# Attention's recurrence in steps of 64 tokens, with all its products in 64x64 quarters of TensorE

## The chip, the cores and the metric

The kernel runs on one core of a Trainium2 chip. The metric is device time in microseconds (us). Of one execution there is also a hardware profile: its span runs from the program's first instruction to its last, and its own time is a little longer than the span.

## The reference

Two blocks follow each other. The first is linear attention with a decay per head (batch 4, 8 heads, 768 tokens, 64 channels a head), the second mixes tokens by a Fourier transform, adds, normalizes, and applies a two-layer MLP. Everything is float32. The part that the change touches is the first block:

```python
for b in range(nb):                       # blocks of 64 tokens
    intra = np.einsum('bhic,bhjc->bhij', qb, kb) * Dmask[None]     # lam ** (i - j), 0 above the diagonal
    intra = np.einsum('bhij,bhjd->bhid', intra, vb)
    inter = np.einsum('bhid,bhde->bhie', qb * lam_pow[None], kv_state)
    out[:, :, sl] = intra + inter
    kb_dec = kb * rev_pow[None]
    kv_state = lam_block[None, :, None, None] * kv_state + np.einsum('bhsd,bhse->bhde', kb_dec, vb)
```

The block length is a matter of arithmetic only: the same outputs come from blocks of 128 tokens. The second block is `u = x + real(fft2(x))`, then `u + relu(norm(u) @ w_ch1) @ w_ch2` with a hidden width of 2048.

## The kernel before

The program is written with a planner: Python emits instructions in an order of priority, and the planner issues on each engine whatever its own estimates of times say is ready, in that priority. `tc.keep_in_program_order` ("pinned") puts an instruction behind the one emitted just before it on the same engine, whatever the estimates say.[...] Generators yield estimated durations, and `weave` uses these to interleave attention, the Fourier part, weight loading and the MLP.

**Front (0 to about 360 us).** Attention goes batch by batch through `attn(b)`, in six chunks of 128 tokens. `attn_in` loads k, q and v of a chunk (L263), scales k by the decay on GpSimd (`kd`, L270), transposes k and q on TensorE (L274, L279) into `kT` and `qT` (ScalarE copies L276, L281), and forms `qs`, q times powers of the decay (VectorE, L285). `attn_out` does the recurrence in four products on TensorE:

- scores, L298: kT by qT for two heads at a time, on 64 rows by 128 columns of the array (two row tiles);
- states, L315: kd by v, 128 rows by 64 columns (two column tiles), added into the running state `st` after a scaling on GpSimd (L319, L320);
- state by qs ("inter"), L328: 64 by 64, the diagonal pair of quarters;
- v by masked scores ("intra"), L332: two column tiles, onto the same PSUM tile as inter.

VectorE multiplies the scores by the decay mask (`sc`, L302). ScalarE copies the result out (`oT`, L335); it is transposed back (L348) and goes on to the Fourier part. Batch 0 also builds a token-reversed copy in `ds` (L341, L390).

Attention's PSUM tiles share a pool of five banks (`psum_a`): scores take two (`pss`), states one (`pu`), the result one (`po`), transposes one each.

The chunks of batches 0 and 1 run beside the conversion of the MLP weights from float64 words (VectorE L217 to L225, ScalarE L216 and L218); those of batches 2 and 3 run beside the plain MLP (first layer L636, second layer L650).

**Late part (about 430 us to the end).** The remaining MLP rows are computed in pairs of row groups by a Strassen-like scheme with seven products a level. `inputs(j)` forms sums of a pair's input tile `ur` on VectorE, B12 at L796 and t1 at L799 among them. `place_sums_w` loads seven stored sums of weights back into the weight tiles (`w<-sd` and `w1s<-sd`, L745); `load_three` loads other stored sums (`tx`, L760), `load_u` the inputs (`ur`, L751), all on SyncE's (SP's) DMA queue. `deep_second(j, k)` are the second layer's seven products (TensorE L1038, read out at L1046 on VectorE and L1044 on ScalarE), `deep_first` the first layer's (L968).

Of the kernel before, what the change touches and what calls it, by code (L numbers as in the profile page):

```python
# [76 lines left out]
def kernel(  # L77
# [13 lines left out]
    DFF = moe_w_ch1.shape[1]  # L91
    C = 128
    NC = S // C
# [63 lines left out]

    decay = const.tile([C, H, C], F32, name="decay")
    for h in range(H):
        scan(decay[:, h, :], lamb[:, h:h + 1].broadcast_to([C, C]), ident, 0.0, op0=ALU.mult, op1=ALU.add)  # L160

    lamq = const.tile([128, HP], F32, name="lamq")
    for hi in range(2):
        nc.vector.tensor_copy(lamq[HD[hi]], lamb[HD[hi], hi::2])
    qpow = const.tile([128, HP, C], F32, name="qpow")
    for hp in range(HP):
        scan(qpow[:, hp, :], lamq[:, hp:hp + 1].broadcast_to([128, C]), ident, 1.0, op0=ALU.mult, op1=ALU.bypass)
    spow = qpow[:, :, C - 1:C]
    kpow = decay[:, :, C - 1:C].broadcast_to([C, H, D])

# [4 lines left out]

    st = [const.tile([128, HP, D], F32, name=f"st{i}") for i in range(2)]

# [81 lines left out]
    def attn_in(b, c):  # L259
# [6 lines left out]

        kd = None
        if c < NC - 1:
            kd = new(at, [C, H, D], "kd")
            nc.gpsimd.tensor_tensor(kd, kt, kpow, op=ALU.mult)  # L270

# [9 lines left out]
        nc.scalar.copy(qT, ptq)  # L281
        qs = None
        if c > 0:
            qs = new(at, [128, HP, C], "qs")
            nc.vector.tensor_tensor(qs, ptq, qpow, op=ALU.mult)  # L285
        ins[b, c] = kT, qT, qs, kd, vt
        yield 1.2

    def attn_out(b, c, head):
# [4 lines left out]
        mm = nc.tensor.matmul  # L294
        pss = [psum_a([C, HP, C]) for _ in range(2)]
        for hp in range(HP):
            for hi in range(2):
                mm(pss[hi][:, hp, :], lhsT=kT[HD[hi], hp, :], rhs=qT[HD[hi], hp, :], start=True, stop=True)  # L298
        sc = []
        for hi in range(2):  # L300
            t = new(at, [C, HP, C], "sc", bufs=3)
            nc.vector.tensor_tensor(t, pss[hi], decay[:, hi::2, :], op=ALU.mult)  # L302
            sc.append(t)
# [3 lines left out]


        s_old, s_new = st[(c + 1) % 2], st[c % 2]
        if not last:  # L310
            pu = psum_a([128, HP, D])
            for hp in range(HP):
                for hi in range(2):
                    h = 2 * hp + hi
                    mm(pu[HD[hi], hp, :], lhsT=kd[:, h, :], rhs=vt[:, h, :], start=True, stop=True)  # L315
            if c == 0:
                nc.vector.tensor_copy(s_new, pu)
            else:
                nc.gpsimd.tensor_tensor(s_new, s_old, spow.broadcast_to([128, HP, D]), op=ALU.mult)  # L319
                nc.vector.tensor_tensor(s_new, s_new, pu, op=ALU.add)  # L320
            yield 0.9


        po = psum_a([128, HP, C])
        if c > 0:
            for hp in range(HP):
                for hi in range(2):
                    mm(po[HD[hi], hp, :], lhsT=s_old[HD[hi], hp, :], rhs=qs[HD[hi], hp, :],  # L328
                       start=(hp == 0), stop=False, skip_group_check=True)
        for hp in range(HP):  # L330
            for hi in range(2):
                mm(po[HD[hi], hp, :], lhsT=vt[:, 2 * hp + hi, :], rhs=sc[hi][:, hp, :],  # L332
                   start=(c == 0 and hp == 0), stop=(hp == HP - 1), skip_group_check=True)
        oT = new(at, [128, HP, C], "oT")
        nc.scalar.copy(oT, po)  # L335
        if b in TURNED:

            if c == 0:
                nc.scalar.copy(first, po[:, :, 0:1])
            elif c > 1:  # L340
                nc.scalar.copy(oTs[b][:, :, 0:1], po[:, :, 0:1])  # L341
        yield 2.0
# [44 lines left out]
        if c > 0:  # L387

            oTs[b] = new(fp, [128, DM + 4], "ds")[:, 0:DM].rearrange("p (h c) -> p h c", h=HP)
            tc.keep_in_program_order(nc.scalar.copy(oTs[b][:, :, C - 1:0:-1], po[:, :, 1:C]))  # L390
        if last:
# [381 lines left out]
    def inputs(j):  # L773
# [21 lines left out]
        B11, B12, B21, B22 = (r[:, :, k::2, m:m + 128] for k in range(2) for m in (0, 128))  # L795
        V.tensor_tensor(B12, B22, B12, op=SUB)  # L796
        yield 0.0
# [224 lines left out]
    def deep_second(j, k):  # L1022
# [32 lines left out]
        if k == 0:  # L1055
# [3 lines left out]
            part_sum(V, h["a11"], h["s1"], h["a11"], SUB)  # L1059
            if j == DEEP - 1:  # L1060
                place_sums_w()
        elif k == 1:
            V.tensor_tensor(y11, y11, T, op=ADD)  # L1063
            add_u(y11, y11, 0, 0)
        elif k == 2:
            if j < DEEP:
                split(h["a22"])
            h["s4"] = h["a12"]
            part_sum(V, h["a12"], h["a12"], h["s2"], SUB)
        elif k == 3:  # L1070
            V.tensor_tensor(y22, y22, T, op=ADD)
            add_u(y21, y22, 1, 0)
            add_u(T, T, 0, 1)
            add_u(y22, y22, 1, 1)
        elif k == 4:
            V.tensor_tensor(y22, y22, y12, op=ADD)
            V.tensor_tensor(y12, y12, T, op=ADD)
        elif k == 5:
            store(*who[1][1], yt[:, 1, 1])
        else:  # L1080
            store(*who[0][1], yt[:, 0, 1])
            store(*who[1][0], yt[:, 1, 0])
            store(*who[0][0], yt[:, 0, 0])
# [181 lines left out]
```

## Time and profile before

| what | us |
|---|---|
| median of three runs | 803.37 |
| the three runs | 800.59, 803.37, 805.32 |
| profiled execution, own time | 800.95 |
| its span | 799.0 |
| TensorE busy | 768.3 |
| VectorE busy | 587.6 |
| ScalarE busy | 217.4 |
| GpSimd busy | 195.0 |

In the profile's rows a line such as L298 names the line of the kernel, `out<-in` the tiles, and `64*128` the rows and columns of the array that a matmul uses. Each float32 matmul leaves two records[...].[...] how fast matmuls follow one another is read from the starts. The granted clock of TensorE was 0.998 over the span.

### The profile page before, as it was taken

The page shows a single profiled execution, that of the slowest core. Times are in us where ns is not written, and L with a number is a line of the kernel's source. Part 1 is how long each engine was busy: PE and PEld are TensorE (multiplying, and loading weights), DVE is VectorE, ACT ScalarE, POOL GpSimd, SP SyncE. Part 2 cuts the span into 40 slices and gives each one's busy share as a digit, 9 for nine tenths or more (in the row PEclk, how much of TensorE's full clock was granted, in tenths as well). Part 3 has the DMA queues.
Part 4 walks back from the last instruction along what each step waited for, and adds up shares of the span by engine and source line. Part 5 has one row for each costly group of instructions (what it writes and reads, how often), then busy time and mean ns, then how long its engine had stood idle before and what let it go on. Part 6 is the DMA issues. An engine that isn't in the chain of part 4 may idle for free.

```text
span 799.0 us, 14578 instructions
## 1 busy us (share of the span) xinstructions
PE 768.3 (96%) x5616; PEld 642.5 (80%) x5616; DVE 587.6 (74%) x1148; ACT 217.4 (27%) x512; POOL 195.0 (24%) x196
## 2 busy tenths in 40 slices
PE   6989999999999999999999999999999999999996
PEld 5768766758675766767846889988899999999995
DVE  6899889675843572246698998769886699758983
ACT  3765443324431221221201221022210342024300
POOL 3213230011111020121003960279204101230021
PEclk9999999999999999999999999999999999999999
DMA  9979724238842137443232375345945555455442
GB/s 229 258 157 246 199 80 130 87 59 214 209 128 87 39 67 154 103 126 100 53 66 93 144 239 159 101 166 194 341 135 148 163 179 177 128 173 187 129 123 77
DMA packets 152331, 116.80 MB, mean 146 GB/s; under 512 B 113998, under 2 KB 113998, under 8 KB 152262
## 3 DMA queue, kind: packets, MB, share of 16 engines
q1 hardware_dynamic: 147120, 103.39, 46.2%
q0 software_dynamic: 2112, 6.69, 2.5%
q10 hardware_dynamic: 3030, 5.78, 2.1%
q8 instruction: 45, 0.74, 0.4%
q14 instruction: 24, 0.20, 0.1%
HBM read 83.58 MB, written 32.25 MB: 145 GB/s over the span
## 4 chain that ended last, share of the span: by engine, by line
PE 77%; DVE 11%; DMA 5%; issue 4%; ACT 1%; POOL 1%; POOLq 0%; ACTq 0%; SPq 0%; DVEq 0%
PE p L1038 20%; PE p L883 12%; PE p L968 11%; PE pm L650 10%; PE pm L636 8%; PE pa L332 3%; PE pa L516 3%; PE pa L298 3%; DMA x<-xb,ix 2%; PE pa L328 2%; DMA w<-sd 1%; PE pa L274 1%; PE pa L315 1%; DVE sc L302 1%; PE pa L348 1%
## 5 line engine op out<-in xcount | busy, mean ns | idle before, releaser
L636 PE MATMUL pm<-ut,w 128*128 128x256 f32 x512 | 119.2, 382 | 0.0
L650 PE MATMUL pm<-w,hr 128*128 128x512 f32 x256 | 115.8, 597 | 0.1
L636 PEld LDWEIGHTS pm<-ut,w 128*128 128x128 f32 x512 | 94.4, 190 | 15.4 <-issue 3.6
L650 PEld LDWEIGHTS pm<-w,hr 128*128 128x128 f32 x256 | 46.6, 190 | 49.5 <-issue 48.0
L1052 POOL TENSOR_TENSOR y<-y,u 128x512 f32<-128x512 f32 x12 | 18.8, 1568 | 200.8 <-DVE y L1063 159.0
L1038 PE MATMUL p<-tx,sx 128*128 128x128 f32 x416 | 54.9, 275 | 0.0
L1038 PEld LDWEIGHTS p<-tx,sx 128*128 128x128 f32 x416 | 50.6, 192 | 0.0
L883 PE MATMUL p<-ur,w 128*128 128x256 f32 x192 | 46.9, 379 | 0.1
L270 POOL TENSOR_TENSOR kd<-k,decay 128x512 f32<-128x512 f32 x20 | 22.6, 1130 | 97.0 <-PE pa L315 53.5
L1046 DVE TENSOR_TENSOR y<-p,y 128x128 f32<-128x128 f32 x92 | 25.4, 287 | 22.2 <-PE p L1038 15.8
L1044 ACT COPY y<-p 128x128 f32<-128x128 f32 x48 | 12.8, 266 | 104.1 <-PE p L1038 103.8
L883 PEld LDWEIGHTS p<-ur,w 128*128 128x128 f32 x192 | 36.3, 190 | 5.7 <-issue 0.5
L302 DVE TENSOR_TENSOR sc<-pa,decay 128x512 f32<-128x512 f32 x48 | 31.5, 684 | 8.7 <-PE pa L298 8.5
L1038 PE MATMUL p<-w,ha 128*128 128x128 f32 x288 | 37.4, 275 | 0.0
L298 PEld LDWEIGHTS pa<-qT,kT 64*128 64x128 f32 x384 | 26.0, 193 | 13.4 <-ACT qT L281 7.5
L332 PE MATMUL pa<-sc,v 128*64 128x128 f32 x384 | 32.2, 286 | 3.5 <-DVE sc L302 3.4
L644 ACT ACTIVATE hr<-pm 128x256 f32<-128x256 f32 x44 | 16.7, 385 | 68.7 <-PE pm L636 68.5
L1038 PEld LDWEIGHTS p<-w,ha 128*128 128x128 f32 x288 | 35.0, 192 | 0.2
L298 PE MATMUL pa<-qT,kT 64*128 64x128 f32 x384 | 30.7, 292 | 3.4 <-ACT qT L281 3.1
L550 POOL TENSOR_SCALAR ve<-mv 128x2 f32<-128x2 f32 x12 | 3.4, 286 | 123.0 <-DVE mv L547 123.0
L883 PE MATMUL p<-sx,w1s 128*128 128x256 f32 x128 | 32.9, 380 | 0.2 <-DVE sx L786 0.2
L332 PEld LDWEIGHTS pa<-sc,v 128*64 128x64 f32 x384 | 23.6, 140 | 11.3 <-DVE sc L302 5.5
(227 smaller groups left out, 1709.8 us busy)
## 6 DMA issues: line engine op xcount, KB each, us to landing
tx<-td SPq DMA_DIRECT2D x84, 256.0 KB, 2.9
raw<-in_moe_w_ch_dram SPq DMA_DIRECT2D x32, 512.0 KB, 5.1
tx<-sd SPq DMA_DIRECT2D x42, 256.0 KB, 2.7
sd<-tx SPq DMA_DIRECT2D x28, 256.0 KB, 2.0
k<-in_k_dram SPq DMA_DIRECT2D x24, 256.0 KB, 5.0
q<-in_q_dram SPq DMA_DIRECT2D x24, 256.0 KB, 5.9
v<-in_v_dram SPq DMA_DIRECT2D x24, 256.0 KB, 4.8
td<-tx SPq DMA_DIRECT2D x21, 256.0 KB, 2.0
```

The lines of the kernel that those rows point to most:

```text
L270: nc.gpsimd.tensor_tensor(kd, kt, kpow, op=ALU.mult)
L298: mm(pss[hi][:, hp, :], lhsT=kT[HD[hi], hp, :], rhs=qT[HD[hi], hp, :], start=True, stop=True)
L302: nc.vector.tensor_tensor(t, pss[hi], decay[:, hi::2, :], op=ALU.mult)
L332: mm(po[HD[hi], hp, :], lhsT=vt[:, 2 * hp + hi, :], rhs=sc[hi][:, hp, :], start=(c == 0 and hp == 0), stop=(hp == HP - 1), skip_group_chec ...
L516: mm = nc.tensor.matmul(ps[0:m, n, :], lhsT=piece(a, i, n), rhs=cs[0:rows, a, i in (2, 3), n, :], start=(a == 0), stop=(a == 1))
L636: nc.tensor.matmul(ps, lhsT=w1[:, c, 128 * fc:128 * fc + 128], rhs=ut[:, c, :], start=(c == 0), stop=(c == KO - 1))
L650: nc.tensor.matmul(ps, lhsT=hr[(fc - f0) // 4][:, fc % 4, 128 * i:128 * i + 128], rhs=w2[:, fc, :], start=(fc == f0), stop=(fc == f1 - 1))
L883: nc.tensor.matmul(ps, lhsT=s2.A[a][:, kt, 128 * i:128 * i + 128], rhs=U[b][:, kt, :], start=(first and kt == 0), stop=(kt == 1), skip_gro ...
L968: nc.tensor.matmul(ps[:, 128 * i:128 * i + 128], lhsT=ab[m][0][:, 128 * i:128 * i + 128], rhs=ab[m][1], start=(start and i == 0), stop=Tru ...
L1038: nc.tensor.matmul(ps[:, 0:HM // 2], lhsT=ab[m][0][i], rhs=ab[m][1][:, i, :], start=(start and i == 0), stop=(i == HF // 2 - 1), skip_grou ...
L1046: V.tensor_tensor(o, ps[:, 0:HM // 2], o, op=ADD)
L1052: nc.gpsimd.tensor_tensor(o, y, u, op=ADD)
```

## The change

The recurrence takes two steps of 64 tokens inside each 128-token chunk; loads, transposes and the copy of oT stay at 128.

- The decay tables cover 64 tokens, and `eye`, the sum of the identity's two halves, takes the identity's place in their scans. There are four state tiles instead of two.
- `kd` is also made for a batch's last chunk, and `qs` also for its first.
- States come first in `attn_out`: half-chunk s uses rows `HD[s]` of kd and v, so all four quarters of the array are used, and both states go into PSUM tiles `ps[0]` and `ps[1]`, beside the place for the scores. Each half's state is the old one scaled on GpSimd plus the sum on VectorE.
- Inter follows, one PSUM tile `po[s]` a half, every matmul pinned; then scores, of which only the two 64x64 blocks on the diagonal are computed, into the other half of `ps[hi]`; the first is pinned behind inter. The masked scores are half as wide.
- Intra uses four quarters as well; oT is copied in two halves, and batch 0's extra copies read oT instead of PSUM.
- In the late part, the sum B12 of `inputs` is pinned, and `place_sums_w()` is emitted after product 2 of the second layer of pair 1 instead of after product 0.

```diff
-    C = 128
+    C, SC = 128, 64
...
-    decay = const.tile([C, H, C], F32, name="decay")
+    decay = const.tile([C, H, SC], F32, name="decay")
     for h in range(H):
-        scan(decay[:, h, :], lamb[:, h:h + 1].broadcast_to([C, C]), ident, 0.0, op0=ALU.mult, op1=ALU.add)
+        scan(decay[:, h, :], lamb[:, h:h + 1].broadcast_to([C, SC]), eye, 0.0, op0=ALU.mult, op1=ALU.add)
...
-        qs = None
-        if c > 0:
-            qs = new(at, [128, HP, C], "qs")
-            nc.vector.tensor_tensor(qs, ptq, qpow, op=ALU.mult)
+        qs = new(at, [128, HP, 2, SC], "qs")
+        nc.vector.tensor_tensor(qs, ptq.rearrange("p h (s i) -> p h s i", s=2),
+                                qpow.broadcast_to([128, HP, 2, SC]), op=ALU.mult)
...
+        ps = [psum_a([128, 2, HP, SC]) for _ in range(2)]
+        for hp in range(HP):
+            for s in range(1 if last else 2):
+                for hi in range(2):
+                    h = 2 * hp + hi
+                    mm(ps[s][HD[hi], 1, hp, :], lhsT=kd[HD[s], h, :], rhs=vt[HD[s], h, :], start=True, stop=True)
+        states = [None if c == 0 else st[(2 * c) % 4]]
+        for s in range(1 if last else 2):
+            old, t = states[-1], st[(2 * c + s + 1) % 4]
+            if old is None:
+                nc.vector.tensor_copy(t, ps[s][:, 1])
+            else:
+                nc.gpsimd.tensor_tensor(t, old, spow.broadcast_to([128, HP, D]), op=ALU.mult)
+                nc.vector.tensor_tensor(t, t, ps[s][:, 1], op=ALU.add)
+            states.append(t)
+        yield 0.9
+
+        po = [psum_a([128, HP, SC]) for _ in range(2)]
+        pin = tc.keep_in_program_order
+        for s in range(2):
+            if states[s] is not None:
+                for hp in range(HP):
+                    for hi in range(2):
+                        pin(mm(po[s][HD[hi], hp, :], lhsT=states[s][HD[hi], hp, :], rhs=qs[HD[hi], hp, s, :],
+                               start=(hp == 0), stop=False, skip_group_check=True))
         for hp in range(HP):
             for hi in range(2):
-                mm(pss[hi][:, hp, :], lhsT=kT[HD[hi], hp, :], rhs=qT[HD[hi], hp, :], start=True, stop=True)
+                for s in range(2):
+                    i = slice(SC * s, SC * s + SC)
+                    m = mm(ps[hi][HD[s], 0, hp, :], lhsT=kT[HD[hi], hp, i], rhs=qT[HD[hi], hp, i], start=True, stop=True)
+                    if hp + hi + s == 0:
+                        pin(m)
         sc = []
         for hi in range(2):
-            t = new(at, [C, HP, C], "sc", bufs=3)
-            nc.vector.tensor_tensor(t, pss[hi], decay[:, hi::2, :], op=ALU.mult)
+            t = new(at, [C, HP, SC], "sc", bufs=4)
+            nc.vector.tensor_tensor(t, ps[hi][:, 0], decay[:, hi::2, :], op=ALU.mult)
             sc.append(t)
...
+        for hp in range(HP):
+            for s in range(2):
                 for hi in range(2):
+                    mm(po[s][HD[hi], hp, :], lhsT=vt[HD[s], 2 * hp + hi, :], rhs=sc[hi][HD[s], hp, :],
+                       start=(states[s] is None and hp == 0), stop=(hp == HP - 1), skip_group_check=True)
+        oT = new(at, [128, HP, C], "oT")
+        for s in range(2):
+            nc.scalar.copy(oT[:, :, SC * s:SC * s + SC], po[s])
...
-        V.tensor_tensor(B12, B22, B12, op=SUB)
+        tc.keep_in_program_order(V.tensor_tensor(B12, B22, B12, op=SUB))
...
-            if j == DEEP - 1:
-                place_sums_w()
         elif k == 1:
...
+            if j == DEEP - 1:
+                place_sums_w()
         elif k == 3:
```

## The prediction

> **What bounds the kernel now.** I read the page's busy times, then the busy times by stage, then the groups by shape, then the order of time inside one chunk.
>
> ```profile
> PE 768.3 (96%) x5616; PEld 642.5 (80%) x5616; DVE 587.6 (74%) x1148; ACT 217.4 (27%) x512; POOL 195.0 (24%) x196
> ```
>
> TensorE (PE) is nearly always busy, but an average hides stages, so I split the front, where attention runs, by time (columns: length, then busy us and instructions of PE, weight load, VectorE (DVE), ScalarE (ACT), GpSimd (POOL)):
>
> ```profile
> 5.00:95.00 90.00, 80.58 (x915) 65.53 (x916) 80.45 (x163) 51.22 (x114) 23.85 (x22) 1.00 0.87 218
> 95.00:140.00 45.00, 43.24 (x197) 30.67 (x198) 39.58 (x97) 17.94 (x43) 11.95 (x9) 1.00 0.41 130
> 140.00:250.00 110.00, 109.06 (x724) 77.89 (x723) 70.79 (x148) 39.64 (x87) 14.41 (x18) 1.00 0.53 137
> 250.00:360.00 110.00, 107.34 (x714) 74.67 (x713) 50.58 (x116) 21.06 (x54) 16.52 (x21) 1.00 0.40 95
> ```
>
> From 5 to 95 us, where batches 0 and 1 run beside the weight conversion, VectorE is as busy as TensorE (80.45 and 80.58 of 90): neither alone sets the pace. From 140 to 360 us, batches 2 and 3 run beside the MLP, TensorE has 216.4 of 220 us and VectorE 121.4. There a microsecond less on TensorE is a microsecond less. This is one full chunk of batch 3, in order of time (start, length first to last, engine, line, shapes, count):
>
> ```profile
> 331.74 1.16 PE L298 MATMUL pa<-qT,kT 64*128 64x128 f32 x16
> 332.83 0.69 PE L315 MATMUL pa<-v,kd 128*64 128x64 f32 x16
> 332.93 1.29 DVE L302 TENSOR_TENSOR sc<-pa,decay 128x512 f32<-128x512 f32 x2 [1.07 <-PE pa L298]
> 333.44 1.09 PE L328 MATMUL pa<-qs,st 64*64 64x128 f32 x16
> 334.13 0.41 DVE L320 TENSOR_TENSOR st<-st,pa 128x256 f32<-128x256 f32 x1
> 334.46 1.09 PE L332 MATMUL pa<-sc,v 128*64 128x128 f32 x16
> 334.69 0.62 POOL L319 TENSOR_TENSOR st<-st,qpow 128x256 f32<-128x256 f32 x1
> 335.49 0.66 PE L274 MATMUL pa<-ident,k 128*128 128x128 f32 x4
> 335.61 0.59 ACT L335 COPY oT<-pa 128x512 f32<-128x512 f32 x1 [3.92 <-PE pa L332]
> ```
>
> The four products take 335.49 − 331.74 = 3.75 us, without a gap: each VectorE step is covered by the next product. Two records stand for one f32 matmul (8 matmuls, 16 records). L315's records last 222 ns (its line's median), so its starts are spread over 0.69 − 0.22 = 0.47 us: 16 records in 8 steps of 58 ns, two at a time. The same sum gives L298 (record 272) 8 steps of 112 and L328 and L332 (269, 273) 8 steps of 109. A matmul on the whole array has no partner:
>
> ```profile
> 613.11 1.06 PE L968 MATMUL p<-ur,w 128*128 128x128 f32 x8
> 614.00 1.06 PE L1038 MATMUL p<-tx,sx 128*128 128x128 f32 x8
> ```
>
> 8 records in 0.89 us, one per 112 ns. So two column tiles (L315, L332), two row tiles (L298) and a diagonal pair (L328) all run at once already. Changing from one product to the next costs more than a step: L315's 0.61 us until L328 starts is 8 × 58 + 0.15; L328's 1.02 and L332's 1.03 are 8 × 109 + 0.15.
>
> [...]
>
> ```profile
> 43.84 1.06 POOL L270 TENSOR_TENSOR kd<-k,decay 128x512 f32<-128x512 f32 x1 [7.71 <-DMA k<-in_k_dram]
> 44.03 1.42 DVE L225 SCALAR_TENSOR_TENSOR w<-w,e 128x512 f32<-128x512 f32 x1
> ```
>
> L225 takes 0.685 us (median of its line), here 1.42.
>
> **The change part by part.** No row shows four quarters at once. I take four records per 58 ns, L315's step, because each pairing of rows and columns already overlaps fully.[...]
>
> *TensorE.* Per full chunk: states 32 records, 8 × 58 = 0.46; state times q uses the two diagonal quarters only, 16 steps × 58 = 0.93; scores 0.46; scores times v 0.46. That is 2.32. Inter and scores stand together, so I count three changes of mode where work lies between, 0.45: 2.77 against 3.75, saving 0.98. Batches 2 and 3, twelve chunks: before 12 × 3.75 − 2 × 1.02 (no L328 in a first chunk) − 2 × 0.61 (no L315 in a last) = 41.7; after 12 × 2.77 − 2 × 0.46 − 2 × 0.23 = 31.9. **−9.8 us.**[...]
>
> *New waits.* The second half's inter needs the state after the first half, and the second score bank is free only when VectorE has read the second state sum out of it, which waits for a GpSimd scaling of the first. With a handover of 0.05 us (L298's end at 332.90, L302 at 332.93): states end on TensorE at 0.52, the last record's tail at 0.69, add (L320, 0.41) to 1.13. Inter 1 may start at 1.19, inter 0 covers to 0.98: 0.2 open. GpSimd (L319, 0.62) and the second add end at 2.3; TensorE is done with inter 1 and half the scores at 1.9: 0.4 open. Then two score multiplies before scores times v; half size, L320's 0.41 each: 0.7 open. Sum 1.3 us per chunk, if nothing lies between. Behind the waiting matmul stands everything on TensorE that the planner put later. But each chunk has transposes of the next (L274 and L279, 0.93) and MLP matmuls (L650, 0.9), and the planner places them by its own estimates, leaving under 4 us of gaps in 220 now. I leave 0.2 a chunk open: **+2.4**, bounds 0 and 12 × 1.3 = 15.6.
>
> *VectorE.* Per batch: 12 score multiplies 0.684 to 0.41, −3.3; one more qs, +0.7; 11 state steps instead of 5, +2.5. About 0. GpSimd: six more scalings and one more kd per batch, 6 × 0.62 + 1.06 = 4.8, off every path except through the blocking: 9.6 us more in 5 to 95, where L225 alone loses 13 × (0.838 − 0.676) = 2.1 us to 23.85 us of GpSimd work. I take +2, bounds 0 and 9.6. ScalarE copies oT in two halves, 2 × 0.39 (L352's size) for 0.59: +0.2 per chunk, also ahead of the turned copies (L341, L390), which then read oT; covered by its idle time (51 of 90 us busy); uncovered, 12 × 0.2 = 2.4. The constants' twelve scans (L160 and L167, 0.4 each) halve and one add is new; VectorE waits 1.2 us for TensorE's first scores after them, so 0; uncovered, −2.2.
>
> *Batches 0 and 1.* TensorE again saves about 10 us, mostly into idle time since VectorE's work stays; where a chunk waits for TensorE it helps a little, and inter now stands ahead of the scores, so the wait for qs is uncovered. I take −1, bounds −6 and +6. With the blocking: **+1**.
>
> *Late part.*
>
> ```profile
> 579.01 0.69 DVE L796 TENSOR_TENSOR ur<-ur 128x512 f32<-128x512 f32 x1 [2.93 <-DMA ur<-utd]
> 579.62 0.28 DVE L1046 TENSOR_TENSOR t<-p,t 128x128 f32<-128x128 f32 x1
> ```
>
> VectorE sits 2.93 us before L796, whose input has not landed; the read of a product (L1046) is queued behind it and TensorE stands 1.44 us. Pinned, the sum goes to its place in the program, near its neighbour L799 at 606, long after the landing. place_sums_w moves seven 256 KB loads (about 0.4 us of issue each) two products later on SP's queue, past the two ur loads and the tx loads of those products, which come some 3 us earlier; the seven are needed near 613, so they have time. **−1.4**, bounds −1.6 and +2 (the seven then delay tx loads).
>
> Sum: −9.8 + 2.4 + 1 − 1.4 = −7.8. The profiled execution took 800.95 us (span 799.0), so about 793; it lies 2.4 under the median of the three runs, 803.37, which I carry over: **795.5**.
>
> **The rivals.** *The handover decides (slower).* If the planner's estimates of quarters are off, the chain PE, DVE, POOL, DVE, PE lies open. Per chunk it is 1.3 us plus about half a VectorE operation of queueing at each of three visits (0.3 each) = 2.2, less 0.98 saved = 1.2; over the 23 chunks after the first, −1.4 for the late part: +26 at worst, half of it +12, 815. It decides once more than 0.98 us a chunk stays open. For it: fixed order on TensorE, one shared bank. Against it: 1.8 us of other TensorE work per chunk. *Quarters don't run four at a time.*[...] 801 to 808, no change. *All is hidden:* stages 140 to 360 save the full 9.8 and batches 0 and 1 gain 5: 787.
>
> **How the numbers follow.** Measurements of this kernel can tell about 0.5% (4 us) from no change. Forecast with the hidden case, 786 to 799: 0.60. No change, 799.4 to 807.4 ([...]half the gain eaten): 0.20. Slower, 808 to 820: 0.20. The range for 8 in 10 is 786 to 812; the forecast's own is 787 to 800.
>
> **What would show it.** Right: records of the states, scores and last product averaging about 15 ns apart (0.7 us per 32), VectorE's score multiplies at 0.41, TensorE still above 98% busy from 140 on with the front ending 8 us earlier, L796's counterpart without an idle time. Wrong: 32 records spread over 0.8 us or more, or idle TensorE ahead of the second inter or the scores, released by the state's add, of over 1 us a chunk.

## The result, and the profile after

The changed kernel takes 835.52 us (median of 6 runs, 833.07 to 838.08) against 803.11 us (6 runs, 800.21 to 805.32): ratio 1.0415, 95% interval 1.0392 to 1.0438. It is slower by 32 us; the forecast was 795.5. The profiled execution took 838.08 us, with a span of 836.3. The times in the table of runs below are medians of executions in the chip's fast state; one of e4's four fell in its slow state and is left out.

The page of after, busy times and the row of granted clock (40 slices, tenths):

```profile
PE 779.9 (93%) x7152; PEld 651.9 (78%) x7152; DVE 587.1 (70%) x1177; ACT 220.0 (26%) x536; POOL 213.1 (25%) x224
PEclk9998899999999998999899999999999999999999
```

VectorE's sum has not moved (587.6 to 587.1), TensorE's share fell from 96 to 93%, and the clock now shows slices at eight tenths in the front.

Three points in time divide the loss: the first matmul of the plain MLP (L636 before, L643 after) comes at 120.6 us instead of 96.9, the first of the late part (L883, L890) at 469.2 instead of 428.9, and the end at 836.3 instead of 799.0. So batches 0 and 1 lose 24 us, batches 2 and 3 beside the MLP 16.6 us, and the late part gains 3.0. Busy time in the first two stages, before and then after (columns: window, length, busy us and count of PE, weight load, VectorE, ScalarE, GpSimd, clock, DMA share, GB/s):

```profile
5.00:96.90 91.90, 82.48 (x932) 67.42 (x933) 80.62 (x163) 52.02 (x117) 25.19 (x23) 1.00 0.88 219
96.90:428.90 332.00, 325.39 (x1886) 227.45 (x1885) 211.23 (x457) 85.45 (x204) 47.26 (x55) 1.00 0.42 109
```

```profile
4.70:120.60 115.90, 90.47 (x1701) 73.69 (x1702) 82.71 (x179) 53.25 (x129) 35.44 (x38) 0.91 0.70 173
120.60:469.20 348.60, 329.53 (x2655) 230.51 (x2654) 209.27 (x471) 86.83 (x216) 55.40 (x69) 0.98 0.40 104
```

VectorE does the same work in the first stage (80.62 and 82.71 us) but in 115.9 us instead of 91.9: its list is not what grew. GpSimd got 10 us more (25.19 to 35.44, still under a third of the stage), and TensorE's busy time rose by 8 us at a lower clock, to 78% of the stage: no engine is full, so they wait for each other. The clock is below 1 in both stages: 20.5 and 13.7 us in all at half clock, where the front of before has none.

This is one chunk of batch 2 of after, in order of time; it answers to the chunk shown of before:

```profile
259.65 0.69 PE L299 MATMUL pa<-v,kd 64*64 64x64 f32 x32
260.17 0.65 PE L317 MATMUL pa<-qs,st 64*64 64x64 f32 x16
260.45 0.42 DVE L307 TENSOR_TENSOR st<-st,pa 128x256 f32<-128x256 f32 x1 [0.50 <-PE pa L299]
260.54 1.06 POOL L270 TENSOR_TENSOR kd<-k,decay 128x512 f32<-128x512 f32 x1 [4.35 <-issue]
261.02 0.59 PE L317 MATMUL pa<-qs,st 64*64 64x64 f32 x13 [0.21 <-DVE st L307]
...
261.55 0.62 POOL L306 TENSOR_TENSOR st<-st,qpow 128x256 f32<-128x256 f32 x1
262.21 0.42 DVE L307 TENSOR_TENSOR st<-st,pa 128x256 f32<-128x256 f32 x1 [1.34 <-POOL st L306]
...
262.69 0.68 PE L323 MATMUL pa<-qT,kT 64*64 64x64 f32 x26 [0.79 <-DVE st L307]
```

The quarters run as fast as forecast: L299's 32 records lie in 0.69 us. But TensorE then waits 0.21 us before the second inter (L317) for the first state sum, and 0.79 us before the scores (L323) for the second one (L307), since the second score bank still holds it. That sum waits 1.34 us for GpSimd, which first does the next chunk's kd (L270, 1.06 us) and only then the scaling (L306). Nothing else of TensorE's list lies in the gap. The whole chunk, from this chunk's transposes of k at 256.16 to the next at 263.30, takes 7.14 us.

The waits of TensorE by what ended them (us in total, times, longest): the main ones of the first stage of before, then those of after before 120.6 us, then those from there to 469.2:

```profile
PE pa L298 <- ACT qT L281: 3.1, 7, 0.7
PE pa L332 <- DVE sc L302: 1.8, 5, 1.0
PE pa L328 <- DVE qs L285: 1.4, 2, 0.8
```

```profile
PE pa L323 <- DVE st L307: 6.1, 8, 1.5
PE pa L338 <- DVE sc L329: 4.9, 8, 1.1
...
PE pa L317 <- DVE qs L283: 2.9, 4, 1.9
PE pa L355 <- ACT ds L348: 2.4, 4, 0.8
PE pa L317 <- DVE st L307: 2.2, 5, 0.8
```

```profile
PE pa L523 <- DVE fe L482: 6.6, 3, 3.5
PE pa L323 <- DVE st L307: 5.7, 8, 0.8
...
PE pa L317 <- DVE st L304: 2.1, 1, 2.1
PE pa L317 <- DVE st L307: 1.2, 6, 0.2
```

To add up the stages I took all starts of TensorE's records in order. A distance of over 350 ns between two starts (700 ns after a 512-column record) counts as lost, less 0.42 ns for each column of the record, an allowance that I set; the rest counts as records. This sees more than the table of waits, which starts at a record's end: one of L299 lasts 0.22 us, while the next starts 15.4 ns later on average.

| TensorE, us | before | after |
|---|---|---|
| to the first MLP matmul: records / lost | 76.4 / 15.5 | 79.9 / 36.0 |
| from there to the late part: records / lost | 323.2 / 8.8 | 319.4 / 29.3 |

The lost time grows by 41 us and makes the whole loss of the front (40 us). The records' own time hardly changes (399.6 to 399.3 us over both stages): the quarters' gain is not to be seen. The allowance is about half of what the trace of before shows (L968 with 128 columns starts a record every 112 ns, L650 with 512 every 429); with the spacing that each line shows, the lost time grows by 38 us, which changes nothing in the reading.

### The profile page after: what moved, and what is told of

Same layout as the page of the kernel before. It is cut to its first block, busy times and chain, and to the rows that moved or that the text cites. A ratio compares the mean times of both kernels' runs of the same rounds, so it can differ in the third digit from the quotient of the medians.

```text
span 836.3 us, 17751 instructions
## 1 busy us (share of the span) xinstructions
PE 779.9 (93%) x7152; PEld 651.9 (78%) x7152; DVE 587.1 (70%) x1177; ACT 220.0 (26%) x536; POOL 213.1 (25%) x224
## 4 chain that ended last, share of the span: by engine, by line
PE 66%; DVE 14%; issue 7%; DMA 5%; POOL 5%; SPq 1%; ACT 1%; POOLq 0%; ACTq 0%; DVEq 0%
PE p L1045 20%; PE p L890 11%; PE p L975 10%; PE pm L643 7%; PE pm L657 5%; PE pa L523 3%; PE pa L338 2%; DMA x<-xb,ix 2%; POOL kd L270 2%; POOL st L306 1%; DVE stt L553 1%; PE pa L323 1%; DVE un L571 1%; POOL rs L558 1%; DVE st L307 1%
## 5 line engine op out<-in xcount | busy, mean ns | idle before, releaser
L657 PE MATMUL pm<-w,hr 128*128 128x512 f32 x256 | 118.6, 603 | 0.1
L643 PE MATMUL pm<-ut,w 128*128 128x256 f32 x512 | 118.2, 385 | 0.0
L643 PEld LDWEIGHTS pm<-ut,w 128*128 128x128 f32 x512 | 96.8, 192 | 16.2 <-issue 4.1
L270 POOL TENSOR_TENSOR kd<-k,decay 128x512 f32<-128x512 f32 x24 | 27.5, 1146 | 142.0 <-issue 49.8
L890 PE MATMUL p<-ur,w 128*128 128x256 f32 x192 | 46.7, 379 | 0.0
L323 PE MATMUL pa<-qT,kT 64*64 64x64 f32 x768 | 30.7, 240 | 11.9 <-DVE st L307 11.8
L283 DVE TENSOR_TENSOR qs<-pa,qpow 128x512 f32<-128x512 f32 x24 | 16.4, 685 | 35.6 <-ACT qT L281 35.3
L1053 DVE TENSOR_TENSOR y<-p,y 128x128 f32<-128x128 f32 x92 | 25.6, 286 | 22.5 <-PE p L1045 15.9
L890 PEld LDWEIGHTS p<-ur,w 128*128 128x128 f32 x192 | 36.4, 190 | 5.3 <-issue 0.5
L317 PE MATMUL pa<-qs,st 64*64 64x64 f32 x704 | 29.8, 226 | 11.1 <-DVE st L307 3.4
L317 PEld LDWEIGHTS pa<-qs,st 64*64 64x64 f32 x704 | 25.0, 137 | 18.8 <-issue 5.8
L306 POOL TENSOR_TENSOR st<-st,qpow 128x256 f32<-128x256 f32 x40 | 28.7, 717 | 41.0 <-DVE st L307 41.0
L323 PEld LDWEIGHTS pa<-qT,kT 64*64 64x64 f32 x768 | 24.6, 147 | 14.5 <-DVE st L307 14.5
L307 DVE TENSOR_TENSOR st<-st,pa 128x256 f32<-128x256 f32 x40 | 16.7, 418 | 26.9 <-POOL st L306 18.7
```

The costliest lines, as they stand in the source:

```text
L306: nc.gpsimd.tensor_tensor(t, old, spow.broadcast_to([128, HP, D]), op=ALU.mult)
L307: nc.vector.tensor_tensor(t, t, ps[s][:, 1], op=ALU.add)
L317: pin(mm(po[s][HD[hi], hp, :], lhsT=states[s][HD[hi], hp, :], rhs=qs[HD[hi], hp, s, :], start=(hp == 0), stop=False, skip_group_check=True))
L323: m = mm(ps[hi][HD[s], 0, hp, :], lhsT=kT[HD[hi], hp, i], rhs=qT[HD[hi], hp, i], start=True, stop=True)
L643: nc.tensor.matmul(ps, lhsT=w1[:, c, 128 * fc:128 * fc + 128], rhs=ut[:, c, :], start=(c == 0), stop=(c == KO - 1))
L657: nc.tensor.matmul(ps, lhsT=hr[(fc - f0) // 4][:, fc % 4, 128 * i:128 * i + 128], rhs=w2[:, fc, :], start=(fc == f0), stop=(fc == f1 - 1))
```

## The experiments

Label, time and ratio to the kernel before on the same chip (95% interval), and the time of the first MLP matmul, with the length of the stage from there to the late part. The last two columns come from one trace each. In e1, whose front is that of the kernel before, they are 1.7 us lower and 1.3 us higher than before (96.9 and 332.0), so differences of 1 to 2 us there tell nothing. Runs e11 to e16 were executed once each, for the times inside their traces, and have no line here.

| run | us | ratio | first MLP | stage after |
|---|---|---|---|---|
| changed kernel | 835.52 | 1.0415 (1.0392 to 1.0438) | 120.6 | 348.6 |
| e1_late_only | 799.57 | 0.9964 (0.9942 to 0.9985) | 95.2 | 333.3 |
| e2_kd_behind | 836.90 | 1.0413 (1.0370 to 1.0457) | 123.5 | 343.0 |
| e3_evac | 824.30 | 1.0244 (1.0162 to 1.0325) | 117.7 | 335.0 |
| e4_spread | 829.43 | 1.0290 (1.0230 to 1.0351) | 120.3 | 345.9 |
| e5_hybrid | 802.02 | 0.9989 (0.9973 to 1.0005) | 96.2 | 336.1 |
| e6_head_first | 822.07 | 1.0251 (1.0234 to 1.0268) | 115.5 | 335.7 |
| e7_piped | 828.76 | 1.0353 (1.0313 to 1.0393) | 116.4 | 341.7 |
| e8_piped_add | 829.08 | 1.0308 (1.0264 to 1.0352) | 119.5 | 340.4 |
| e9_filler | 849.14 | 1.0558 (1.0515 to 1.0601) | 134.7 | 345.5 |
| e10_piped_filler | 828.67 | 1.0317 (1.0275 to 1.0359) | 120.7 | 338.9 |
| e17_filler_128 | 834.83 | 1.0412 (1.0388 to 1.0436) | 119.3 | 345.5 |
| e18_piped_filler_256 | 832.89 | 1.0376 (1.0352 to 1.0400) | 123.0 | 343.2 |

My theory was a chain of handovers inside each chunk (TensorE, VectorE, GpSimd, VectorE, TensorE) that TensorE cannot cover. The rivals: four quarters lower the clock by themselves; the added GpSimd work only blocks VectorE; the number of PSUM banks; TensorE's half clock as a cost of its own.

**The late part alone.** The kernel before with this edit and the call of `place_sums_w()` two products later:

```diff
-        V.tensor_tensor(B12, B22, B12, op=SUB)
+        tc.keep_in_program_order(V.tensor_tensor(B12, B22, B12, op=SUB))
```

> The kernel before with only the late part's two edits (the sum B12 pinned, the stored weight sums loaded two products later). Theory 'late part as predicted, attention lost the rest': about 801.5, 1.4 to 1.6 us under the kernel before, B12 without an idle time ahead of it. Rival 'the late part's gain comes only with the new front': 803, no difference, and B12's wait goes to another row.

Measured 799.57 us, 2.9 us under the kernel before by the ratio (interval 1.2 to 4.7). The stretch from the first late matmul to L968's first fell from 184.2 to 182.5 us, in the changed kernel to 182.7. So the late part does what was forecast, 1.5 to 1.7 us of it visible in the trace, and the attention part lost the rest. **This is the version that beats both kernels**, the kernel before by 0.4%.

**Who holds the second score bank.** First only the order on GpSimd:

```diff
-        nc.gpsimd.tensor_tensor(kd, kt, kpow, op=ALU.mult)
+        tc.keep_in_program_order(nc.gpsimd.tensor_tensor(kd, kt, kpow, op=ALU.mult))
```

> The changed kernel with the scaling of k (kd) pinned on GpSimd behind the second scaling of the state, nothing else. Theory 'chain': a kd of 1.06 us stands ahead of the second scaling, so the second score bank opens about 1 us later than it could; with kd behind, the 14.2 us that TensorE loses before the scores fall under 5, and the time falls by 8 to 15 us, to 820 to 827. Rival 'quarters or clock': stalls are not what costs, time stays at 835 within 2 us. Rival 'GpSimd only moves the wait': kd comes late, TensorE waits before the states instead, 830 to 840.

The waits of TensorE over the front of that run:

```profile
PE pa L338 <- DVE sc L329: 9.7, 12, 1.6
PE pa L299 <- POOL kd L270: 9.5, 4, 4.8
...
PE pa L323 <- DVE st L307: 2.2, 10, 0.4
```

The scores' wait went as expected, from 11.8 to 2.2 us, and came back as 9.5 us before the states (kd is late now) and 4.8 us more before the last product. Time 836.90: the third theory named there was right. kd's place alone is not the cause; with either order someone waits. So GpSimd was taken out of TensorE's way:

```diff
-            else:
+            elif s == 0:
                 nc.gpsimd.tensor_tensor(t, old, spow.broadcast_to([128, HP, D]), op=ALU.mult)
                 nc.vector.tensor_tensor(t, t, ps[s][:, 1], op=ALU.add)
+            else:
+                u1 = new(at, [128, HP, D], "u1")
+                nc.scalar.copy(u1, ps[s][:, 1])
+                nc.gpsimd.tensor_tensor(t, old, spow.broadcast_to([128, HP, D]), op=ALU.mult)
+                nc.gpsimd.tensor_tensor(t, t, u1, op=ALU.add)
```

> The changed kernel, but the second state sum is copied out of PSUM by ScalarE as soon as it is there, and scaled and added on GpSimd from SBUF, so no bank waits for GpSimd. Theory 'chain': the wait before the scores goes (14.2 us to under 3), time 812 to 825; GpSimd does about 15 us more work, some of it against VectorE. Rival 'clock': the half-clock stretches come from the quarters themselves, clock stays at 0.98, 828 to 836. Rival 'blocking': GpSimd's added work slows VectorE, 835 or more.

The windows of that run:

```profile
4.70:117.70 113.00, 89.56 (x1700) 74.05 (x1701) 85.05 (x169) 56.14 (x137) 44.56 (x48) 0.88 0.70 176
117.70:452.70 335.00, 321.79 (x2655) 224.29 (x2654) 206.18 (x461) 90.42 (x226) 63.61 (x79) 1.00 0.42 109
```

The wait before the scores is gone from the second stage, its length falls from 348.6 to 335.0 us (before: 332.0), its clock is back at 1.00, and a dense chunk takes 5.94 us instead of 7.14. So in batches 2 and 3 the second score bank, with the half clock that came with it, is 13.6 of the 16.6 us (the edit also takes one add a chunk from VectorE). The rival "four quarters lower the clock by themselves" falls: this stage runs all its attention in quarters at full clock. So does "the added GpSimd work only blocks VectorE": GpSimd has more to do here than in the changed kernel, 63.61 against 55.40 us, in a shorter stage. But the first stage gained only 2.9 us: there the wait moved on to the masked scores (TensorE's longest wait before 117.7 us; last product, released by VectorE):

```profile
PE pa L343 <- DVE sc L334: 13.5, 9, 2.5
```

TensorE's order was then changed as well: inter of the first half, scores of one head of each pair, inter of the second half, scores of the other head.

```diff
+        for t in range(2):
...
+            hi = t
+            for hp in range(HP):
+                for s in range(2):
+                    i = slice(SC * s, SC * s + SC)
+                    m = mm(ps[1 - hi][HD[s], 0, hp, :], lhsT=kT[HD[hi], hp, i], rhs=qT[HD[hi], hp, i], start=True, stop=True)
```

> As the one before (second sum copied out by ScalarE), and TensorE's order is state times q of the first half, scores of one head of each pair (into the bank that ScalarE empties), state times q of the second half, scores of the other head. Theory 'chain': the wait before the second inter is covered as well; only the wait for the masked scores stays, 0.7 us a chunk: 803 to 815, clock back at 0.99 or more. Rival 'clock': still 828 or more with a clock of 0.98. Rival 'VectorE's queue in batches 0 and 1 is what costs': the gain is small before 140 us and the first MLP matmul still starts after 115 us, 820 to 828.

It missed: 829.43 us, with a clock of 0.969 in its trace. These are the numbers that the clock rival gave, but e3's second stage had already run quarters at full clock, and waits show here too. In the first stage the scores now wait for ScalarE's copy (L310), which stands in ScalarE's list behind other copies:

```profile
PE pa L343 <- DVE sc L334: 9.1, 8, 3.3
PE pa L328 <- ACT u L310: 6.0, 6, 1.7
```

In the second stage a matmul of the MLP waited 4.3 us for a weight tile, against 0.2 in e3. It seems that moving a few matmuls in one list shifted the others; that was not tried apart.

**Which batches.** Both recurrences in one kernel: batches 0 and 1 in steps of 128, batches 2 and 3 as in e3, the late part as changed.

```diff
+    OLD = (0, 1)
+    def attn_in(b, c):
+        return (in_128 if b in OLD else in_64)(b, c)
```

> Batches 0 and 1 take the recurrence of the kernel before (steps of 128), batches 2 and 3 that of the kernel with the second sum copied out by ScalarE; the late part as changed. Theory 'the early loss is the chain of handovers inside each chunk of batches 0 and 1': the first MLP matmul comes back to 94 to 99 us (120.6 changed, 117.7 with the copy), the stage from there to the late part stays at 333 to 337, no half-clock stretch in front; time 800 to 804. Rival 'tables, loads or weights delay the early part': first MLP matmul after 110 us, 815 or more.

The windows of that run:

```profile
5.00:96.20 91.20, 81.24 (x933) 65.94 (x934) 81.26 (x166) 51.79 (x117) 24.97 (x23) 1.00 0.89 222
96.20:432.30 336.10, 324.21 (x2655) 227.37 (x2654) 205.80 (x461) 90.16 (x225) 63.94 (x79) 0.99 0.42 108
```

As the theory expected: the first stage is back at 91.2 us and full clock, the second at 336.1, the time at 802.02. So the 24 us of the first stage come from the recurrence in batches 0 and 1; its batch 0 makes the token-reversed copy into ds from oT as the changed kernel does, so that copy is not the cause. The run also has decay tables of 128 tokens again. Those are made once, ahead of the first chunk, while the changed kernel falls behind through all twelve: the scores of the 1st, 4th, 8th and 12th chunk start 2.0, 8.4, 15.1 and 25.6 us later than before. And the new recurrence, freed of its bank wait, still gains nothing where TensorE is the limit: 336.1 against 332.0 us.

**What holds batches 0 and 1.** These kernels start from e3, but for the controls e14 and e15. First the next chunk's transposes between scores and last product:

```diff
         yield 1.5
+        yield from head
...
         oT = new(at, [128, HP, C], "oT")
...
         yield 2.0
-        yield from head
```

> The kernel with the second sum copied out by ScalarE, and the next chunk's loads and transposes emitted between the scores and the last product, so that they are at hand while VectorE masks the scores. Theory 'chain': the wait before the last product (15.0 us of lost time there) falls under 6, 812 to 817. Rival 'the planner had put the transposes there already': 822 to 826, the wait stays.

822.07 us, the rival's value, though not for its reason: the wait before the last product did go (16.2 to 0.6 us lost in the first stage), but TensorE then waited 8.3 us before q's transposes and 14.3 us, instead of 5.9, before the transposition of the result.

The states a whole chunk ahead, in PSUM tiles of their own, so that nobody waits for a state inside its chunk; e8 keeps the add on VectorE:

```diff
     def attn_in(b, c):
...
+        ps = [psum_a([128, HP, SC]) for _ in range(2)]
...
+        ins[b, c] = kT, qT, qs, vt, states
```

> One chunk of lead: the states of the next chunk are computed with its transposes, between the scores and the last product of this chunk, in PSUM tiles of their own; the second sum copied out by ScalarE. Then no state is waited for inside a chunk, and the masking of the scores is covered by transposes and states. Theory 'chain': lost time before inter, scores and last product under 10 us in all, clock 1.0 in front, first MLP matmul at 88 to 96, time 790 to 802. Rival 'quarters lower the clock': clock 0.98, 815 or more. Rival 'banks': two more PSUM tiles in flight of five make the transposes wait, 803 to 815.

> As the one before, but the second state is added on VectorE from PSUM after GpSimd's scaling, as in the changed kernel. Theory 'chain': nobody on TensorE waits for that add any more, so within 3 us of the one before, rather faster (GpSimd 15 us less work). Rival 'banks': the sum holds its bank until GpSimd is done, 5 us or more slower than the one before.

The order of e6 is in both. e7 missed: 828.76 us, the first MLP matmul at 116.4 instead of 88 to 96. e8 did as expected against e7: 829.08 us, so the sum that holds its bank for GpSimd costs nothing there. TensorE's waits in the first stage in e7, and in e13, the same kernel with seven PSUM banks for attention instead of five:

```profile
PE pa L279 <- DVE sc L336: 8.1, 6, 2.2
PE pa L362 <- ACT oT L350: 6.1, 6, 2.3
PE pa L362 <- ACT ds L356: 5.7, 4, 2.3
```

```profile
PE pa L346 <- DVE sc L336: 8.7, 7, 2.3
PE pa L362 <- ACT oT L350: 5.5, 6, 1.3
```

```diff
-    pa = psums.enter_context(tc.tile_pool(name="pa", bufs=5, space=PS))
-    pm = psums.enter_context(tc.tile_pool(name="pm", bufs=3, space=PS))
+    pa = psums.enter_context(tc.tile_pool(name="pa", bufs=7, space=PS))
+    pm = psums.enter_context(tc.tile_pool(name="pm", bufs=1, space=PS))
```

> The kernel with the states one chunk ahead, with seven PSUM banks for attention's tiles instead of five, and one instead of three for the MLP (which slows the MLP; only the time up to the first MLP matmul is compared, 116.4 with five banks). Theory 'banks took the place of the state chain': TensorE's 10 us of waits before q's transposes go to under 3 and the first MLP matmul comes at 95 to 106. Rival 'VectorE's and ScalarE's lists set the pace': 112 to 118.

> The changed kernel with seven banks for attention and one for the MLP. The scores still share their banks with the states, so theory 'handover inside the chunk' expects little before the first MLP matmul: 116 to 122 (120.6 with five). Rival 'it was the number of banks all the time': under 108.

> Control: the kernel before with seven banks for attention and one for the MLP. First MLP matmul at 94 to 98 (96.9 with five) if banks were not short there; 85 to 92 if they were.

First MLP matmul at 113.4 (e13), 120.9 (e14) and 98.1 us (e15). With seven banks q's transposes no longer wait for the masked scores, and the same 8 us of that wait stand before the last product: e13 came at the rival's value. The number of banks is not the cause: neither the changed kernel nor the kernel before came earlier with seven. Last, the second inter of e3 takes the chunk's first state:

```diff
-                        pin(mm(po[s][HD[hi], hp, :], lhsT=states[s][HD[hi], hp, :], rhs=qs[HD[hi], hp, s, :],
+                        pin(mm(po[s][HD[hi], hp, :], lhsT=(states[0] or states[1])[HD[hi], hp, :], rhs=qs[HD[hi], hp, s, :],
```

> The kernel with the second sum copied out by ScalarE, whose second inter uses the chunk's first state instead of the state after the first half (so the outputs are not the reference's): TensorE waits for no state of its own chunk. Theory 'each handover counts': the first MLP matmul comes 3 to 8 us earlier than the 117.7 with that wait, and the stage after it is 2 to 5 us shorter than 335.0. Rival 'the wait only moves to the masking of the scores': both within 2 us.

First MLP matmul at 116.7 us, 1.0 earlier than in e3; the stage after it got longer (340.0 us, with 13.7 us at half clock, none in e3). Taken away alone, this wait, too, brought no gain.

**VectorE's other work.** 14 tiles of weights are not converted; another load of 256 KB stands in the place of each:

```diff
+        if len(skipped) < 14:
+            skipped.append(0)
+            nc.sync.dma_start(dst.rearrange("p (h d) -> p h d", h=H), k[0, :, 0:C, :].rearrange("h p d -> p h d"))
+            return
```

> The kernel before, in which the first 14 tiles of weights are not converted: a load of 256 KB of other data stands in their place, so the outputs are not the reference's and VectorE and ScalarE have that work no more. Theory 'VectorE sets the pace of batches 0 and 1 (92.0 us busy in 91.9)': the first MLP matmul comes at 78 to 88 instead of 96.9. Rival 'it is attention's own chain': 93 to 97.

> The changed kernel with the same tiles left unconverted (outputs not the reference's). Theory 'each added handover waits in VectorE's list behind conversion work': without that work the first MLP matmul comes within 8 us of the kernel before without conversion (24 us with it), 80 to 92 us. Rival 'the chain alone': still 15 us or more behind the kernel before without conversion. Rival 'clock': the gap stays and half-clock stretches stay.

The first windows of e11 and of e12:

```profile
5.00:91.70 86.70, 78.55 (x932) 65.60 (x933) 49.78 (x98) 35.81 (x91) 20.43 (x24) 1.00 0.94 197
```

```profile
4.70:104.50 99.80, 85.80 (x1700) 70.46 (x1701) 50.49 (x114) 36.80 (x103) 30.54 (x38) 0.93 0.79 168
```

Without 31 us of VectorE's work the kernel before gains only 5 us: VectorE did not set the pace there; the result is on the rival's side, a little beyond it. That attention's own chain sets it is argued, not shown: TensorE is busy in 78.55 of the 86.7 us, and the DMA engines' share is 0.94. The changed kernel gains 16. The gap falls from 24.0 to 13.1 us: some 11 us of the loss appear only beside the conversion work, as they would if handovers stand behind it in VectorE's list; 13 us remain without it, the chain with the 13.7 us of half clock that it still has (clock 0.93). My "within 8 us" was too small.

**The half clock.** A product of two constants into a PSUM tile nobody reads, in batches 0 and 1 only: e9, on the changed kernel, has it ahead of scores, last product and transposition of the result; e10, on e7, ahead of q's transposes, inter and transposition of the result.

```diff
+    def filler(b):
+        if b < 2:
+            tc.keep_in_program_order(nc.tensor.matmul(psum_m([128, H * SC]), lhsT=ident, rhs=decay.rearrange("p h i -> p (h i)"), start=True, stop=True))
```

> The changed kernel with idle work on TensorE in batches 0 and 1: a product of two constants, into a PSUM tile that nobody reads, 0.43 us at full clock, ahead of the scores, of the last product and of each transposition of the result (some 40 of them, 17 us of work, meant to lie in the 36 us that TensorE waits there). Theory 'the half clock is a cost of its own': the half-clock stretches before the first MLP matmul (20.5 us) go to under 7, and that matmul comes at 108 to 118 instead of 120.6, although work was added. Rival 'the half clock costs nothing, the waits set the pace': it comes at 119 to 124 whatever the clock. Rival 'TensorE is short there': it comes after 130.

> The kernel with the states one chunk ahead (copied out by ScalarE), with the same idle work on TensorE in batches 0 and 1, ahead of q's transposes, of inter and of each transposition of the result. Theory 'half clock': 34 us of half clock before the first MLP matmul go to under 10, that matmul comes at 98 to 110 instead of 116.4. Rival 'waits set the pace': 115 to 121.

Such a product took 0.87 us, not the 0.43 I had put down: two records of 0.43 each. Half clock before the first MLP matmul fell from 20.5 to 6.8 us (e9) and from 34.1 to 3.4 us (e10), and that matmul came at 134.7 and 120.7 us, each at the value of a rival (TensorE is short there; the waits set the pace). The other records of TensorE shrank in e9 from 79.9 to 105.0 − 36.3 = 68.7 us, but 36 us of idle work stood in the way. So again, smaller (only the columns change; e17 on the changed kernel, e18 with 256 columns on e7):

```diff
-            tc.keep_in_program_order(nc.tensor.matmul(psum_m([128, H * SC]), lhsT=ident, rhs=decay.rearrange("p h i -> p (h i)"), start=True, stop=True))
+            tc.keep_in_program_order(nc.tensor.matmul(psum_m([128, 128]), lhsT=ident, rhs=decay.rearrange("p h i -> p (h i)")[:, 0:128], start=True, stop=True))
```

> The changed kernel with the idle product ahead of scores, last product and transposition of the result in batches 0 and 1, but 128 columns wide, so 0.22 us each (40 of them, 9 us) instead of the 0.87 us that the 512-column ones took. The wide ones removed the half clock before the first MLP matmul (20.5 to 6.8 us) and brought attention's own records from 79.9 us to 105.0 - 36.3 = 68.7, but cost more than they saved. Theory 'half clock is a cost of its own, some 10 us': half clock under 10 us, first MLP matmul at 108 to 116 (120.6 without filler), time 824 to 832. Rival 'the waits set the pace whatever the clock': 119 to 127. Rival 'too little to keep the clock': half clock stays over 15 us and nothing is told.

> The kernel with the states one chunk ahead, with 256-column idle products (0.43 us each, 39 of them, 17 us) instead of 512. With 512 columns half clock went from 34 to 3.4 us and the first MLP matmul came at 120.7, with 34 us of idle work, against 116.4 without. Theory 'half clock': half clock under 10 us and the first MLP matmul at 104 to 112. Rival 'waits set the pace': 115 to 121.

The first window of e17:

```profile
5.00:119.30 114.30, 97.15 (x1781) 79.54 (x1782) 81.22 (x177) 52.69 (x130) 34.05 (x38) 0.97 0.68 175
```

In e17 the clock is 0.97 instead of 0.91 (6.8 us at half), yet the first MLP matmul comes at 119.3 instead of 120.6 and the time is the changed kernel's: the rival "the waits set the pace whatever the clock". By the count above, the other records fell by 5.1 us (79.9 to 74.8) and the lost time by 9.2 us (36.0 to 26.8), while the idle products take 12.9 us. So 13.7 us less at half clock shortened these records by about 5 us, against the 24 us that the stage lost: the half clock looks more like a sign of the waiting than like its cause. e9 has the same half clock, so its 68.7 us are not the clock's doing alone. How much of the 5 us would come through to the end without idle work in the way is not shown. In e18 half clock fell only from 34.1 to 20.5 us and the first MLP matmul came at 123.0 instead of 116.4: it does not decide this.

**What stays open:** how the 13 us of bare chain in batches 0 and 1 divide. Taking handovers away gave back at most 7.5 us (several at once, from e14 to e13: 116.2 to 108.7 us of stage length); single ones gave 1 to 3 us (e3, e6, e16) or made the stage longer (e2, e4), and the next wait took the place of the last. The Fourier part's wait for VectorE (L516 before, L523 after) grew from 3.2 to 8.9 us lost, and stayed at 6.9 in e3; why was not tried.

## Why the prediction was wrong

- **The bound.** "There a microsecond less on TensorE is a microsecond less" held only while nothing new was waited for; and for batches 0 and 1, "neither alone sets the pace" was right for VectorE, as e11 shows, and should have warned that waits set it.
- **TensorE's saving, −9.8: right in kind, too large.** The four products of the second stage took 13.99 + 6.02 + 10.21 + 13.36 = 43.6 us before (41.7 in the sum), in e3 7.67 + 10.38 + 8.57 + 9.25 = 35.9 (31.9 in the sum). The four-quarter step is right: L299's 32 starts span 0.477 us, 15.4 ns each, 58 for each four after the first. What was missed seem to be changes from one product to another (0.15 us each in the trace of before; the forecast calls them changes of mode, and that none lies between inter and scores was my estimate). This is read from the order in the chunks, and no run tests it: the planner cut the last product in two around two of q's transposes, and the transposes, 16.3 us before, took 19.0. Net −5.0 instead of −9.8.
- **New waits, +2.4: the step that failed.** The mechanism was named rightly, its size was not: the open size of three waits was put at 1.3 us a chunk "if nothing lies between". Then 0.2 was taken, since transposes and MLP matmuls would be put there. In the trace they stand elsewhere: between inter and scores there is nothing, and the second bank alone costs 0.79 us in the chunk shown, twice the 0.4 of the sum, since kd stands ahead of the scaling. Lost time in the stage of batches 2 and 3 grew by 20.5 us: the scores' bank 7.2 and inter 4.9, together 12.1 against the forecast 2.4, inside its bound of 15.6; and the Fourier part 5.7 and the MLP 2.7, waits that the sum did not have at all. The third wait, for the masked scores, did not grow there (1.8 us lost before, 0.8 after).
- **Batches 0 and 1, +1 with bounds −6 and +6 for the chain: +24.** The sum had taken VectorE's and TensorE's shares, not the number of times that one waits for the other. With the added visits and half clock, lost time grew by 20.5 us, and the quarters' gain does not show in the records (76.4 before, 79.9 after), of which half clock accounts for some 5 us (e17).
- **VectorE and GpSimd blocking, +2:** the size is a coincidence. VectorE's busy time in the first stage grew by 2.1 us (80.62 to 82.71), with 16 instructions more, but the line that the forecast named took less time: the 13 runs of L225 there took 10.9 us before and 9.9 after (L227). What the forecast calls blocking is three of those 13 runs of before, 1.22 to 1.42 us long, each beside kd on GpSimd (L270). The other ten took 0.68 to 0.69 us, three of them beside GpSimd work too: that GpSimd's work slows VectorE in general is not shown.
- **Late part, −1.4: right.** −1.5 to −1.7 in the traces up to L968, −2.9 (−4.7 to −1.2) by whole executions (e1). Up to the end the traces show −2.5 (e1) and −3.0, but e11, with this part as before, also has −1.5, so the rest is not shown. The sum now stands in its place without an idle time:

```profile
647.09 0.68 DVE L803 TENSOR_TENSOR ur<-ur 128x512 f32<-128x512 f32 x1
```

- **The rivals.** "The handover decides" was the one that came, with the mechanism as described, at 20% and up to +26. But 835.5 us lies above even that, and the slowest range that was given a chance ended at 820, short of that rival's own worst case. Its price of 1.2 us a chunk for 23 chunks was too low: the front lost 40.3 us, 1.75 a chunk. It left out the half clock (20.5 and 13.7 us in the two stages) and the waits of the Fourier part and the MLP (5.7 and 2.7 us more in the second). "Quarters don't run four at a time" is excluded by the starts, 15.4 ns apart on average; its 801 to 808 us was my estimate and is not shown by any trace.

## What to carry to other kernels

Making TensorE's pieces shorter pays only if what they covered stays covered: count the visits to other engines between two products before and after, and price each with what stands ahead of it in that engine's list, not with the operation alone (here kd's 1.06 us on GpSimd stood ahead of the scaling, and VectorE waited 1.34 us for it). A saving and a new wait in the same chain are not weighed by sums of busy time; where an average shows two engines at 88 to 90% each, look at the chain. When one wait is taken away and the time stays (e2, 836.90 us after 835.52), the next was nearly as long: take the whole change back in one part (as e5 did) before you repair it piece by piece.

## What the runs showed of the hardware that I had not expected

- TensorE's granted clock fell to half in six stretches of 3.4 or 6.8 us in the changed kernel's front. In the 3.4 us ahead of each, records covered 35 to 62% of the time, and the longest distance between two starts was 0.87 to 2.1 us before the four in batches 0 and 1 (2.7 and 3.9 us before the two later ones). The starts of the six lie whole multiples of 3.41 us apart. A share of records does not settle it alone: the changed kernel lost its clock after a window with 62% (18.7 to 22.1 us) and kept it after one with 44% (288.4 to 291.8 us). What decides stays open. A little idle work (e17) left one stretch of 6.8 us before the first MLP matmul, of four with 20.5 us.
- Four 64x64 tiles together start a record every 15.4 ns on average (L299, 32 starts in 0.477 us): 6 or 7 ns apart within a four, mostly 38 or 39 from one four to the next. Two tiles do so every 31 ns by the same count (L315 before, 16 starts in 0.464 us): 6 or 7 ns apart within a pair, mostly 51 or 52 from pair to pair. Between these two lines, the float32 product in four quarters starts records at about twice the rate of the one in two tiles.
